# The last 96-point stage of an FFT filter in 64x64 tiles inside batched visits

## The chip, the cores and the metric

One core of one Trainium2 chip runs the kernel. The metric is device microseconds (us) of one execution. Every time below is in us unless it says ns. Engines are called as in the profile: PE or TensorE (matmul), PEld (its weight loads), DVE (VectorE), ACT (ScalarE), POOL (GpSimd) and SP (SyncE, which here only issues DMAs).

## The reference

```python
X = np.fft.rfft(x, axis=1)                  # x: 8 x 3072 x 256
y = np.fft.irfft(X * (filt_r + 1j * filt_i), n=3072, axis=1)
x = y.reshape(8 * 3072, 256)
h1, h2 = x @ w1, x @ w2                     # 256 -> 1024
out = np.maximum(h1, h2) @ w_out            # 1024 -> 256
```

The kernel uses max(h1, h2) = relu(x (w1 - w2)) + x w2, so the second part is out = relu(y Wd) Wo + y M with Wd = w1 - w2 and M = w2 w_out.

## The kernel before, in words

The transform of length 3072 is split as 96 x 32. For each of 8 batches there are four stages. s1 takes 96-point transforms along the first index, already as sums and differences of two halves of 48 (fold, on POOL, makes those from an fp32 load, load_xf); its result goes to DRAM (ad) and is read back transposed (bt, by s1_read). s2 does the 32-point part with the tables U, product multiplies by the filter on DVE, s3 goes back with the tables VP and VQ; its result goes to DRAM (zd) and is read back (zr, by z_read). s4 is the last stage, a 96-point transform for 4 of the 32 columns m, and makes one tile y_ of 384 points x 256 features, as two halves of 128 features. In before it is 8 matmuls of the stationary zr (96 x 128) with the moving table G1 (96 x 96).

The main loop runs over 64 tiles tt = 8 b + i, each of 8 steps j. A step has moe_h (two matmuls of 384 columns into one PSUM tile ph, and a ReLU into gt on ACT or DVE), and then 3 or 4 matmuls of moe_o for the tile before (into po, in another PSUM pool of two banks), whose result two blocks at a time is copied to ot on DVE and sent to DRAM by two DMAs on POOL's queue. **A step is named by its number 8 i + j in its batch, 0 to 63.** The tiles ph, pz, px, pa, py all come from one PSUM pool of six banks.

The order is written by hand and each engine keeps to it. While batch b goes through the loop, the stages s1 to s3 of later batches are done in visits, at steps listed by hand (mid: ahead of the step's moe_o; todo: behind it). A visit for number n does s3 of n-1, s2 of n, some s1 (a "quad" is one s1: four matmuls in 64x64 tiles of the array, a term I use for any such four), and the two products of n. plan_f2 lists, for each batch, the steps of the visits, of load_xf and fold, of both z_read (half h of the z rows) and of s1_read. s4(tt + 1) is called behind step 4 (6 for the last tile of a batch) of tile tt. SP's queue has all the DMAs of load_xf, s1 (ad), s1_read (bt), s3 (zd) and z_read (zr) in program order; a DMA that waits for data holds up those behind it.

In batch 0 the first stages are done in another way (s1t, t1, s3t, t2), with zr made by transposes.

Of the kernel before, what the change touches and what calls it, by code (L numbers as in the profile page):

```python
# [8 lines left out]
FP32 = mybir.dt.float32  # L9
BF16 = mybir.dt.bfloat16  # L10
AF = mybir.ActivationFunctionType
OP = mybir.AluOpType

B = 8
N = 3072
D = 256
# [4 lines left out]
NU = 24  # L21
TWO_PI = 6.283184
RND = 12582912.0


@with_exitstack
def kernel(
# [26 lines left out]
    M = const.tile([128, 2, D], BF16)  # L54
    I128 = const.tile([128, 128], BF16)
    NI = const.tile([128, 128], BF16)
    W1 = const.tile([128, 512], BF16)
    zT = const.tile([128, 2, NM, NU, 4], BF16)
    w2b = const.tile([128, 2, HID], BF16)
    w2T = const.tile([128, 8, D], BF16)  # L60

# [284 lines left out]
    def s1(b, c):  # L346
        if c == 0:
            ad[b] = dram.tile([96, NM, D], BF16, tag="ad", name="ad")
        if c % 2 == 0:
            at_[b] = apool.tile([128, 8, D], BF16, tag="at", name="at")  # L350
        at = at_[b]
        pa = [ps.tile([128, 2, D], FP32, tag="ps", name="pa%d" % g) for g in range(2)]
        for g, r in ((0, 0), (1, 1), (0, 1), (1, 0)):
            TE.matmul(pa[g][64 * r:64 * r + 64], CT[64 * g:64 * g + 64, r], xb[b, c][64 * g:64 * g + 64, r],  # L354
                      start=True, stop=True)
        for g in range(2):
            m0 = 4 * (c % 2) + 2 * g
            S.activation(at[:, m0:m0 + 2], pa[g], AF.Copy)  # L358
        if c % 2 == 1:
            for r in range(2):  # L360
                nc.sync.dma_start(out=ad[b][48 * r:48 * r + 48, 4 * c - 4:4 * c + 4], in_=at[64 * r:64 * r + 48])
# [6 lines left out]

    def z_read(b, h):
        if h == 0:  # L370
            zr[b] = zrpool.tile([96, NM, D], BF16, tag="zr", name="zr")
        src = zd[b][12 * h:12 * h + 12].rearrange("u (q m) d -> (u q) m d", q=4)
        for m in range(0, NM, 8):
            nc.sync.dma_start(out=zr[b][48 * h:48 * h + 48, m:m + 8], in_=src[:, m:m + 8])

    def s2(b, v):
        px = [ps.tile([128, 2, D], FP32, tag="ps", name="px%d" % s) for s in range(2)]
# [20 lines left out]
    def s3(b, v, pq):  # L398
        if v == 0:
            zd[b] = dram.tile([NU, 128, D], BF16, tag="zd", name="zd")  # L400
        pz = [ps.tile([128, 2, D], FP32, tag="ps", name="pz%d" % g) for g in range(2)]
        for i in range(2):
            for q, tab in enumerate((VP, VQ)):
                for g, s in ((0, 0), (1, 1), (0, 1), (1, 0)):
                    TE.matmul(pz[g][64 * s:64 * s + 64, i], tab[64 * g:64 * g + 64, 2 * v + i, s],  # L405
                              pq[s][64 * g:64 * g + 64, q, i], start=(q == 0), stop=(q == 1))
        zt = zpool.tile([128, 2, 2, D], BF16, tag="zt", name="zt")
        for g in range(2):
            S.activation(zt[:, :, g], pz[g], AF.Copy)  # L409
        nc.sync.dma_start(out=zd[b][4 * v:4 * v + 4].rearrange("u p d -> p u d"),  # L410
                          in_=zt.rearrange("p i g d -> p (i g) d"))
# [3 lines left out]
    def visit(b, n, quads):  # L415
# [7 lines left out]
        if n < 6:  # L423
            pend[b, n] = [product(V, n, s, px[s]) for s in range(2)]

    yt = {}

    def s4(tt):
        b, i = divmod(tt, 8)
        y_ = ypool.tile([128, 2, 384], BF16, tag="yt", name="y_")  # L430
        for dc in range(2):
            py = ps.tile([128, 4, NP], FP32, tag="ps", name="py")
            for m in range(4):
                TE.matmul(py[:, m], zr[b][:, 4 * i + m, 128 * dc:128 * dc + 128], G1, start=True, stop=True)  # L434
            o_ = y_[:, dc].rearrange("p (t m) -> p t m", m=4)
            i_ = py.rearrange("p m t -> p t m")
            if dc == 0:
                S.activation(o_, i_, AF.Copy, scale=1.0 / 1536.0)
            else:
                V.tensor_scalar(o_, i_, 1.0 / 1536.0, None, OP.mult)  # L440
        yt[tt] = y_
# [3 lines left out]
            if (j in (1, 4, 6) if 2 < 8 * i + j < 11 else j in (1, 2, 4, 6, 7) if 8 * i + j < 22  # L445
                else (j in (1, 5) and (i, j) != (3, 1)) or (i, j) == (3, 0) if 8 * i + j < 48 else j in (1, 3, 6))}

    def moe_h(tt, j):
        if j == 0:
            gt[tt] = gpool.tile([128, 8, 384], BF16, tag="gt", name="gt")  # L450
        y_ = yt[tt]
        ph = ps.tile([128, 384], FP32, tag="ps", name="ph")
        for dc in range(2):
            TE.matmul(ph, Wd[:, dc, 128 * j:128 * j + 128], y_[:, dc], start=(dc == 0), stop=(dc == 1))  # L454
        if (tt, j) in on_v if tt < 8 else j in (1, 3, 6):
            V.tensor_scalar(gt[tt][:, j], ph, 0.0, None, OP.max)  # L456
        else:
            S.activation(gt[tt][:, j], ph, AF.Relu)  # L458
# [14 lines left out]
    def moe_o(tt, k0, k1):  # L473
        y_, g_ = yt[tt], gt[tt]
        for k in range(k0, k1):
            c, e = divmod(k, 10) if tt else FIRST[k]
            n = e if tt else (e + 2) % 10
            q = 3 * tt + c
            blk = slice(128 * c, 128 * c + 128)
            if e == 0 and (q % 2 == 0 or q == 24 * B - 1):  # L480
                po[q // 2 % 2] = pso.tile([128, 2, D], FP32, tag="po", name="po")
            p_ = po[q // 2 % 2][:, q % 2]
            if n < 2:
                TE.matmul(p_, y_[:, n, blk], M[:, n], start=(e == 0), stop=(e == 9))  # L484
            else:
                TE.matmul(p_, g_[:, n - 2, blk], Wo[:, n - 2], start=(e == 0), stop=(e == 9))  # L486
            if e == 9 and q >= 24 * B - 2:
                e = q % 6
                if q % 2 == 0:
                    S.activation(ot[tt // 2][:, e], p_, AF.Copy)  # L490
                else:
                    S.activation(ot[tt // 2][:, e, 0:112], p_[:, 0:112], AF.Copy)
                    V.tensor_copy(ot[tt // 2][:, e, 112:D], p_[:, 112:D])
                out_block(tt, c)
            elif e == 9 and q % 2 == 1:
                if q % 6 == 1:
                    ot[tt // 2] = opool.tile([128, 6, D], FP32, tag="ot", name="ot")
                e = q % 6
                V.tensor_copy(ot[tt // 2][:, e - 1:e + 1], po[q // 2 % 2])  # L499
                for qq in (q - 1, q):  # L500
                    out_block(qq // 3, qq % 3)

# [80 lines left out]
    for c in range(8):  # L583
# [5 lines left out]
        if c < 7:  # L589
            spin(2)  # L590
    bt[0] = bpool.tile([128, NU, D], BF16, tag="bt", name="bt")
    for n in range(6):
        t1(n, S if n % 2 else V)
    put_v(0, 0, table_v(0, 0))
# [60 lines left out]
    apool = ctx.enter_context(tc.tile_pool(name="apool", bufs=3))  # L655
    zpool = ctx.enter_context(tc.tile_pool(name="zpool", bufs=3))
    opool = ctx.enter_context(tc.tile_pool(name="opool", bufs=2))
    ypool = ctx.enter_context(tc.tile_pool(name="ypool", bufs=3))
    gpool = ctx.enter_context(tc.tile_pool(name="gpool", bufs=2))
    f1(1, 0, S)  # L660
    spin(1)
# [10 lines left out]
    def plan(b, step, fn, *a):  # L672
        todo.setdefault((b + step // 64, step % 64), []).append((fn, a))
# [8 lines left out]
    def plan_f2(b, steps, quads, xs, folds):  # L682
        for n, st in enumerate(steps):
            mid.setdefault((b, st), []).append((visit, (b + 1, n, quads[n])))
        plan(b, steps[3] + 3, z_read, b + 1, 0)
        plan(b, steps[6] + 3, z_read, b + 1, 1)
        if b + 2 < B:
            for c in range(8):
                plan(b, xs[c], load_xf, b + 2, c)
                plan(b, folds[c], fold, b + 2, c)  # L690
            plan(b, steps[-1] + (6 if b else 11), s1_read, b + 2)
# [4 lines left out]
    for c, n in ((2, 7), (4, 22), (5, 32), (6, 40), (7, 48)):  # L696
        plan(0, n, t2, c, (V,))
    plan_f1(0, 1, (5, 6, 7, 7, 10, 10, 11, 11, 12, 12, 13, 13), 14)
    plan_f2(0, (25, 28, 31, 35, 38, 42, 46), ((0,), (), (1,), (2,), (3,), (4,), (5, 6)),
            (8, 10, 15, 18, 21, 27, 30, 33), (16, 19, 25, 28, 31, 34, 38, 42))  # L700
    for b in range(1, B - 1):
        plan_f2(b, (14, 18, 23, 31, 34 if b < B - 2 else 35, 39, 47), ((0,), (1,), (2,), (3,), (4,), (5,), (6, 7)),
                range(-25, 31, 7), range(-14, 42, 7) if b > 1 else range(-15, 41, 7))

    mid[0, 50] = [(visit, (1, 7, (7,)))]

    mid[0, 8] = [(t2, (3, (V,))), (prep_t, (1,))]

    for tt in range(8 * B + 1):
        b, i = divmod(tt, 8)  # L710
        k = 0
        for j in range(8):
            step = 8 * i + j
            if tt < 8 * B:
                moe_h(tt, j)
            for fn, a in mid.get((b, step), ()):
                fn(*a)
            if tt > 0:
                n = 3 if j in (3, 7) else 4
                moe_o(tt - 1, k, k + n)  # L720
                k += n
            for fn, a in todo.get((b, step), ()):
                fn(*a)
            if j == (6 if i == 7 else 5 if tt == 3 else 4) and tt + 1 < 8 * B:
                s4(tt + 1)


# [28 lines left out]
```

## Time and profile before

| | us |
|---|---|
| median of 3 runs | 501.48 (499.88 to 501.93) |
| span of the profiled execution, first to last instruction | 499.6 |
| what the runs have around that span | 0.3 to 2.3, by the median 1.9 |
| TensorE busy in the span | 486.2 |
| DVE, ACT, POOL busy | 329.9, 309.0, 258.7 |
| steps 0 to 63 of batch 0, 1, 2 and 6 | 63.4, 57.5, 57.1, 55.3 |

The profiled execution's own time is not listed apart from its span, so the median stands for it. A timeline row has the start, the length, the engine, the line, the operation, the tiles written and read, the shape and the count of merged instructions; in brackets the idle time of its engine before it and what ended that. In the chain of waits a row is one piece of the chain that ended last. For a matmul the length is from its start to the landing of its result, and the next one starts long before that.

### The profile page before, as it was taken

How to read it: one execution, taken by the hardware profiler on the slowest of the kernel's cores; microseconds unless marked ns; L12 is line 12 of the kernel's file. 1: busy time of each engine (PE TensorE's matmuls, PEld its weight loads, DVE VectorE, ACT ScalarE, POOL GpSimd, SP SyncE). 2: the span in 40 equal slices, each digit the busy share in tenths (PEclk: the TensorE clock that was granted, in tenths of full speed). 3: DMA queues.
4: the chain of work that ended last, by engine and by line, in shares of the span. 5: the costliest groups of instructions: out<-in, count | busy, mean ns of one | idle time of the engine just before them, and what ended most of it. 6: DMA issues, size and time to landing. Idle time of an engine off the chain costs nothing.

```text
span 499.6 us, 13073 instructions
## 1 busy us (share of the span) xinstructions
PE 486.2 (97%) x5297; PEld 361.0 (72%) x5300; DVE 329.9 (66%) x515; ACT 309.0 (62%) x630; POOL 258.7 (52%) x342
## 2 busy tenths in 40 slices
PE   7689999999999999999999999999999999999996
PEld 3457767777777777777777777777777777777775
DVE  7786788458865578457865678557774588555552
ACT  5777478647774577646775577646676456544442
POOL 8795569637546584539547394438642221222220
PEclk9989999999999999999999999999999999999999
DMA  8989799997689768896489776896677625521112
GB/s 130 159 236 219 216 245 298 277 258 210 206 241 245 206 202 219 257 261 195 150 252 251 197 231 189 261 261 181 199 205 206 158 85 149 172 83 64 64 64 85
DMA packets 78046, 97.23 MB, mean 195 GB/s; under 512 B 8065, under 2 KB 54434, under 8 KB 77954
## 3 DMA queue, kind: packets, MB, share of 16 engines
q1 hardware_dynamic: 64786, 66.80, 50.5%
q0 software_dynamic: 13200, 29.60, 20.7%
q8 instruction: 41, 0.67, 0.6%
q14 instruction: 19, 0.16, 0.1%
HBM read 53.87 MB, written 47.19 MB: 202 GB/s over the span
## 4 chain that ended last, share of the span: by engine, by line
PE 83%; DMA 11%; POOL 3%; SPq 1%; DVE 1%; issue 1%; ACT 0%; POOLq 0%
PE po L486 32%; PE ph L454 30%; PE po L484 8%; PE pz L405 4%; PE py L434 4%; DMA zd<-zt 2%; DMA bt<-ad 2%; DMA WS<-in_moe_w_dram 2%; PE px L381 2%; PE pa L354 2%; DMA xb<-in_x_dram 2%; POOL F L121 1%; DMA ad<-at 1%; POOL xb L88 1%; DMA F<-in_filt_i_dram 1%; DMA zr<-zd 1%
## 5 line engine op out<-in xcount | busy, mean ns | idle before, releaser
L486 PE MATMUL po<-Wo,gt 128*128 128x256 bf16 x1536 | 261.1, 273 | 0.0
L458 ACT ACTIVATE gt<-ph 128x384 bf16<-128x384 f32 x321 | 157.6, 495 | 146.8 <-PE ph L454 145.7
L486 PEld LDWEIGHTS <-gt 128*128 128x128 bf16 x1536 | 146.0, 98 | 66.7 <-issue 12.0
L467 POOL DMA_DIRECT2D out_dram<-ot x186 | 102.7, 557 | 170.8 <-DVE ot L499 166.4
L456 DVE TENSOR_SCALAR gt<-ph 128x384 bf16<-128x384 f32 x191 | 104.5, 553 | 64.3 <-PE ph L454 60.7
L387 DVE TENSOR_TENSOR pq<-px,F 128x1024 bf16<-128x1024 f32 x91 | 106.9, 1219 | 26.4 <-PE px L381 26.2
L454 PEld LDWEIGHTS <-Wd 128*128 128x128 bf16 x1024 | 96.5, 98 | 12.2 <-issue 0.3
L103 POOL TENSOR_TENSOR xb<-XF 128x512 bf16<-128x512 f32 x48 | 61.2, 1275 | 52.8 <-DMA XF<-in_x_dram 52.0
L499 DVE COPY ot<-po 128x512 f32<-128x512 f32 x95 | 65.2, 686 | 24.9 <-PE po L486 24.8
L104 POOL TENSOR_TENSOR xb<-XF 128x512 bf16<-128x512 f32 x48 | 60.9, 1269 | 0.0
L358 ACT ACTIVATE at<-pa 128x512 bf16<-128x512 f32 x96 | 51.8, 612 | 4.6 <-PE pa L354 4.6
L409 ACT ACTIVATE zt<-pz 128x512 bf16<-128x512 f32 x84 | 45.6, 595 | 4.9 <-PE pz L405 0.8
L434 PE MATMUL py<-G,zr 96*128 96x96 bf16 x512 | 32.6, 206 | 0.1
L434 PEld LDWEIGHTS <-zr 96*128 96x128 bf16 x512 | 28.9, 97 | 2.4 <-DVE zr L563 0.6
L405 PE MATMUL pz<-pq,VP 64*64 64x256 bf16 x336 | 22.0, 281 | 0.0
L381 PE MATMUL px<-bt,U 64*64 64x256 bf16 x384 | 20.2, 278 | 1.3 <-ACT VQ L278 0.7
L405 PE MATMUL pz<-pq,VQ 64*64 64x256 bf16 x336 | 21.0, 269 | 0.0
L405 PEld LDWEIGHTS <-VP 64*64 64x64 bf16 x336 | 9.9, 105 | 13.3 <-issue 13.0
L354 PE MATMUL pa<-xb,CT 64*64 64x512 bf16 x192 | 18.1, 377 | 0.3 <-DVE y__1495 L440 0.3
L381 PEld LDWEIGHTS <-U 64*64 64x64 bf16 x384 | 10.5, 108 | 4.2 <-issue 3.6
L570 PE MATMUL pd<-W 128*128 128x512 bf16 x28 | 10.1, 474 | 1.5 <-DVE zero L149 1.5
L405 PEld LDWEIGHTS <-VQ 64*64 64x64 bf16 x336 | 10.0, 106 | 0.0
(428 smaller groups left out, 602.9 us busy)
## 6 DMA issues: line engine op xcount, KB each, us to landing
out_dram<-ot POOLq DMA_DIRECT2D x186, 128.0 KB, 3.7
XF<-in_x_dram SPq DMA_DIRECT2D x96, 192.0 KB, 4.6
ad<-at SPq DMA_DIRECT2D x56, 192.0 KB, 3.7
zd<-zt SPq DMA_DIRECT2D x42, 256.0 KB, 3.1
zr<-zd SPq DMA_DIRECT2D x56, 192.0 KB, 4.6
bt<-ad SPq DMA_DIRECT2D x13, 768.0 KB, 10.5
WS<-in_moe_w_dram SPq DMA_DIRECT2D x4, 512.0 KB, 8.1
xb<-in_x_dram POOLq DMA_DIRECT2D x8, 192.0 KB, 6.6
```

What stands on the lines that cost most here:

```text
L103: G.tensor_tensor(t_[:, 0], f[:, 0], f[:, 1], OP.add)
L104: G.tensor_tensor(t_[:, 1], f[:, 0], f[:, 1], OP.subtract)
L358: S.activation(at[:, m0:m0 + 2], pa[g], AF.Copy)
L387: E.tensor_tensor(pq, px.rearrange("p (o i) d -> p o i d", o=1).to_broadcast([128, 2, 2, D]), F[:, :, 2 * v:2 * v + 2, s], OP.mult)
L405: TE.matmul(pz[g][64 * s:64 * s + 64, i], tab[64 * g:64 * g + 64, 2 * v + i, s], pq[s][64 * g:64 * g + 64, q, i], start=(q == 0), stop=(q ...
L434: TE.matmul(py[:, m], zr[b][:, 4 * i + m, 128 * dc:128 * dc + 128], G1, start=True, stop=True)
L454: TE.matmul(ph, Wd[:, dc, 128 * j:128 * j + 128], y_[:, dc], start=(dc == 0), stop=(dc == 1))
L456: V.tensor_scalar(gt[tt][:, j], ph, 0.0, None, OP.max)
L458: S.activation(gt[tt][:, j], ph, AF.Relu)
L467: E.dma_start(out=dst, in_=ot[tt // 2][:, 3 * (tt % 2) + c])
L486: TE.matmul(p_, g_[:, n - 2, blk], Wo[:, n - 2], start=(e == 0), stop=(e == 9))
L499: V.tensor_copy(ot[tt // 2][:, e - 1:e + 1], po[q // 2 % 2])
```

## The change

s4 of tiles 8 to 63 becomes s4f. The 96 points are split into two halves of 48 (by the parity s of the frequency), which zr now holds on partitions 0 to 47 and 64 to 111; z_read writes them with two DMAs where there was one. Each half is transformed with a table G2 of 48 x 48, in 64x64 tiles of the array, 32 matmuls of 48 columns for a tile, into two PSUM tiles pc. ACT copies the one to ce, and DVE writes the sum and the difference of ce and the other to y_. The scale 1/1536 goes to the output copy. s4f is called in the visits (visit_y), ahead of s1, s3 and s2. A batch has ten visits from batch 2 on, at other steps than before; the steps of load_xf, fold, z_read and s1_read move as well, the ReLUs are dealt out anew between ACT and DVE (relu_on_v), and zT moves into the pool of bt. Batch 0 keeps s4 and its own plan, and gets table_g2 and a visit at step 61.

```diff
+SCALE = 1.0 / 1536.0
...
+    G2 = const.tile([128, 64], BF16)
     W1 = const.tile([128, 512], BF16)
-    zT = const.tile([128, 2, NM, NU, 4], BF16)
...
     def z_read(b, h):
         if h == 0:
-            zr[b] = zrpool.tile([96, NM, D], BF16, tag="zr", name="zr")
-        src = zd[b][12 * h:12 * h + 12].rearrange("u (q m) d -> (u q) m d", q=4)
+            zr[b] = zrpool.tile([128, NM, D], BF16, tag="zr", name="zr")
+        src = zd[b][12 * h:12 * h + 12].rearrange("u (s r m) d -> s u r m d", s=2, r=2)
         for m in range(0, NM, 8):
-            nc.sync.dma_start(out=zr[b][48 * h:48 * h + 48, m:m + 8], in_=src[:, m:m + 8])
+            for s in range(2):
+                nc.sync.dma_start(out=zr[b][64 * s + 24 * h:64 * s + 24 * h + 24, m:m + 8],
+                                  in_=src[s][:, :, m:m + 8])
...
+    def table_g2():
+        pg = ps.tile([128, 64], FP32, tag="ps", name="pg2")
+        for s in range(2):
+            TE.matmul(pg[64 * s:64 * s + 64], CT[0:64, s], I128[0:64, 0:64], start=True, stop=True)
+        S.activation(G2, pg, AF.Copy)
+
     yt = {}
+
+    def s4f(tt):
+        b, i = divmod(tt, 8)
+        y_ = ypool.tile([128, 2, 384], BF16, tag="yt", name="y_")
+        pc = [ps.tile([128, 2, 4, 48], FP32, tag="ps", name="pc%d" % s) for s in range(2)]
+        for dc in range(2):
+            for m in range(4):
+                for s, h in ((0, 0), (1, 1), (0, 1), (1, 0)):
+                    d0 = 128 * dc + 64 * h
+                    TE.matmul(pc[s][64 * h:64 * h + 64, dc, m], zr[b][64 * s:64 * s + 48, 4 * i + m, d0:d0 + 64],
+                              G2[64 * s:64 * s + 48, 0:48], start=True, stop=True)
+        ce = cepool.tile([128, 2, 48, 4], FP32, tag="ce", name="ce")
+        S.activation(ce, pc[0].rearrange("p c m t -> p c t m"), AF.Copy)
+        for k, op in enumerate((OP.add, OP.subtract)):
+            V.tensor_tensor(y_[:, :, 192 * k:192 * k + 192].rearrange("p c (t m) -> p c t m", m=4),
+                            ce, pc[1].rearrange("p c m t -> p c t m"), op)
+        yt[tt] = y_
+
+    def visit_y(b, n, tiles, quads):
+        for tt in tiles:
+            s4f(tt)
+        for c in quads[1:]:
+            s1(quads[0], c)
+        if n is not None and n > 0:
+            s3(b, n - 1, pend.pop((b, n - 1)))
+        if n is not None and n < 6:
+            px = s2(b, n)
+            pend[b, n] = [product(V, n, s, px[s]) for s in range(2)]
 
     def s4(tt):
         b, i = divmod(tt, 8)
@@ -445,6 +482,19 @@
             if (j in (1, 4, 6) if 2 < 8 * i + j < 11 else j in (1, 2, 4, 6, 7) if 8 * i + j < 22
                 else (j in (1, 5) and (i, j) != (3, 1)) or (i, j) == (3, 0) if 8 * i + j < 48 else j in (1, 3, 6))}
 
+    def relu_on_v(tt, j):
+        if tt < 8:
+            return (tt, j) in on_v
+        b, i = divmod(tt, 8)
+        step = 8 * i + j
+        if b == B - 1 or b == B - 2 and step > 43:
+            return j in (1, 3, 6)
+        if step < 3 or step > 42:
+            return j % 2 == 1
+        if b == 1 and step < 10:
+            return j % 2 == 1
+        return step in ((10, 15, 20, 26, 32, 37) if b == 1 else (3, 10, 16, 22, 28, 35, 40))
+
     def moe_h(tt, j):
         if j == 0:
             gt[tt] = gpool.tile([128, 8, 384], BF16, tag="gt", name="gt")
@@ -452,7 +502,7 @@
         ph = ps.tile([128, 384], FP32, tag="ps", name="ph")
         for dc in range(2):
             TE.matmul(ph, Wd[:, dc, 128 * j:128 * j + 128], y_[:, dc], start=(dc == 0), stop=(dc == 1))
-        if (tt, j) in on_v if tt < 8 else j in (1, 3, 6):
+        if relu_on_v(tt, j):
             V.tensor_scalar(gt[tt][:, j], ph, 0.0, None, OP.max)
         else:
             S.activation(gt[tt][:, j], ph, AF.Relu)
...
-                V.tensor_copy(ot[tt // 2][:, e - 1:e + 1], po[q // 2 % 2])
+                if tt < 8:
+                    V.tensor_copy(ot[tt // 2][:, e - 1:e + 1], po[q // 2 % 2])
+                else:
+                    V.tensor_scalar(ot[tt // 2][:, e - 1:e + 1], po[q // 2 % 2], SCALE, None, OP.mult)
...
+    zT = bpool.tile([128, 2, NM, NU, 4], BF16, tag="bt", name="zT")
...
-    ypool = ctx.enter_context(tc.tile_pool(name="ypool", bufs=3))
+    ypool = ctx.enter_context(tc.tile_pool(name="ypool", bufs=4))
+    cepool = ctx.enter_context(tc.tile_pool(name="cepool", bufs=2))
...
+    mid[0, 50] = [(visit, (1, 7, (7,)))]
+    plan(0, 44, table_g2)
+    mid[0, 61] = [(visit_y, (1, None, (8,), ()))]
+
+    def at(b, st, tiles=(), quads=(), n=None):
+
+        if b + st // 64 >= 0:
+            mid.setdefault((b + st // 64, st % 64), []).append((visit_y, (b + 1, n, tiles, quads)))
+
     for b in range(1, B - 1):
-        plan_f2(b, (14, 18, 23, 31, 34 if b < B - 2 else 35, 39, 47), ((0,), (1,), (2,), (3,), (4,), (5,), (6, 7)),
-                range(-25, 31, 7), range(-14, 42, 7) if b > 1 else range(-15, 41, 7))
-
-    mid[0, 50] = [(visit, (1, 7, (7,)))]
+        t = 8 * b
+        nb = b + 2 if b + 2 < B else None
+        if b == 1:
+            at(b, 4, (t + 1,), (3, 0, 1))
+            at(b, 10, (t + 2,), (3, 2), 0)
+            at(b, 15, (), (3, 3), 1)
+            at(b, 20, (t + 3,), (), 2)
+            at(b, 26, (t + 4,), (), 3)
+            at(b, 32, (t + 5,), (), 4)
+            at(b, 37, (), (3, 4), 5)
+            at(b, 43, (t + 6,), (3, 5), 6)
+            at(b, 47, (), (3, 6, 7))
+            z0, z1, read = 30, 46, 52
+            folds = range(-15, 41, 7)
+        else:
+            early = b == 2
+            s3_, s22, s40 = ((nb, 3), (nb, 4), (nb, 5)) if early else ((nb, 4), (nb, 5), ())
+            at(b, 3, (t + 1,), s3_ if nb else (), 0)
+            at(b, 10, (t + 2,), (), 1)
+            at(b, 16, (t + 3,), (), 2)
+            at(b, 22, (), s22 if nb else (), 3)
+            at(b, 28, (t + 4,), (), 4)
+            at(b, 35, (t + 5,), (), 5)
+            if nb:
+                at(b, 40, (), s40, 6)
+                at(b, 43, (t + 6,), (nb, 6, 7))
+            else:
+                at(b, 43, (t + 6, t + 7), (), 6)
+            z0, z1, read = 26, 44 if nb else 46, 49
+            folds = range(-23, 33, 7) if early else range(-31, 25, 7) if b == 3 else range(-35, 29, 8)
+        if nb:
+            more = b + 3 < B
+            first = b + 1 == 2
+            at(b, 51, (t + 7,), ((b + 3, 0) if first else (b + 3, 0, 1)) if more else ())
+            at(b, 59, (t + 8,), ((b + 3, 1, 2) if first else (b + 3, 2, 3)) if more else ())
+        else:
+            at(b, 59, (t + 8, t + 9))
+        plan(b, z0, z_read, b + 1, 0)
+        plan(b, z1, z_read, b + 1, 1)
+        if nb:
+            for c in range(8):
+                plan(b, folds[c] - 11, load_xf, nb, c)
+                plan(b, folds[c], fold, nb, c)
+            plan(b, read, s1_read, nb)
+    for k in (2, 4, 6):
+        at(B - 1, 8 * k - 5, (8 * B - 8 + k, 8 * B - 7 + k))
...
             if j == (6 if i == 7 else 5 if tt == 3 else 4) and tt + 1 < 8 * B:
-                s4(tt + 1)
+                if tt + 1 < 8:
+                    s4(tt + 1)
```

More of the change, by code (lines that the diff above doesn't have):

```diff
@@ L489, in moe_o @@
                 if q % 2 == 0:
-                    S.activation(ot[tt // 2][:, e], p_, AF.Copy)
+                    S.activation(ot[tt // 2][:, e], p_, AF.Copy, scale=SCALE)
                 else:
-                    S.activation(ot[tt // 2][:, e, 0:112], p_[:, 0:112], AF.Copy)
-                    V.tensor_copy(ot[tt // 2][:, e, 112:D], p_[:, 112:D])
+                    S.activation(ot[tt // 2][:, e, 0:112], p_[:, 0:112], AF.Copy, scale=SCALE)
+                    V.tensor_scalar(ot[tt // 2][:, e, 112:D], p_[:, 112:D], SCALE, None, OP.mult)
                 out_block(tt, c)
```

## The prediction

> **What bounds the kernel now.** I read the page first, parts 1 and 4.
>
> ```profile
> PE 486.2 (97%) x5297; PEld 361.0 (72%) x5300; DVE 329.9 (66%) x515; ACT 309.0 (62%) x630; POOL 258.7 (52%) x342
> PE 83%; DMA 11%; POOL 3%; SPq 1%; DVE 1%; issue 1%; ACT 0%; POOLq 0%
> ```
>
> TensorE is busy for 97% of the span and carries 83% of the chain. The view by windows says where it isn't: in the steady batch from 159.0 to 216.1 it is busy for 57.10 us of 57.10, at clock 1.00. DVE has 38.07 there and ACT 37.12. So from batch 1 on every microsecond of TensorE work, and every wait put in front of it, moves the end; ACT and DVE count only through when they free something. Next, the timeline of TensorE around one visit and one s4 (start, length; a matmul's length is latency, its cost is the distance to the next start):
>
> ```profile
> 230.77 0.49 PE L454 MATMUL ph<-y__4292,Wd 128*128 128x384 bf16 x2
> 231.19 0.30 PE L405 MATMUL pz<-pq,VP 64*64 64x256 bf16 x4
> 231.32 0.28 PE L405 MATMUL pz<-pq,VQ 64*64 64x256 bf16 x4
> 231.65 0.39 PE L381 MATMUL px<-bt,U 64*64 64x256 bf16 x8
> 231.87 0.39 PE L354 MATMUL pa<-xb,CT 64*64 64x512 bf16 x4
> 232.19 0.39 PE L486 MATMUL po<-Wo,gt 128*128 128x256 bf16 x2
> ...
> 234.05 0.51 PE L434 MATMUL py<-G,zr 96*128 96x96 bf16 x8
> 234.39 0.49 PE L454 MATMUL ph<-y__4292,Wd 128*128 128x384 bf16 x2
> ```
>
> An s4 costs 0.34 (234.05 to 234.39). A visit pays for the change of tile form: the ph pair takes 0.33, so the first pz was due at 231.10 and came 0.09 late; its first four take 0.13 where later fours take 0.11; the pa quad takes 0.215, so po was due at 232.085 and came 0.10 late. That is 0.22 a visit. s3 is 0.46, later 0.44 (without the 0.02), s2 0.22, one s1 0.22.
>
> Small 64x64 tiles stand in the start-up, also at clock 1.00:
>
> ```profile
> 18.70 0.38 PE L264 MATMUL pv<-I,U 64*64 64x64 bf16 x24
> 18.91 0.27 PE L381 MATMUL px<-bt,U 64*64 64x256 bf16 x1
> ```
>
> Six quads with 64 moving columns take 0.21: 35 ns a quad.
>
> **The change, part by part.** Scale: the profiled execution has a span of 499.6, the median of the runs is 501.48, so 1.9 lies around the span; I put differences on the median.
>
> *TensorE's own work.* 56 tiles (8 to 63) give up an s4 of 0.34 for 8 quads of 48 columns. Upper price 35 ns a quad (L264's row, wider by a third): 0.28. Lower: two px quads of 256 columns take 0.22, so 0.43 ns a column, 21 ns a quad, 0.17. I take L264 by its columns, 48/64 x 35 = 26 ns, 0.21, since that row has the tile form. Gain 56 x 0.13 = 7.3 (3.4 to 9.5). Against it, visits go from 50 (8 + 6 x 7) to 71 (9, 11, 4 x 10, 8, 3 by batch): 21 x 0.22 = 4.6, and table_g2 changes form once more, 0.2. Sum -2.5 (+1.4 to -4.7). The Trainium skill, "TensorE: Matmul & The Clock Gate", section LDWEIGHTS, gives a weight load as columns over 1.2 per ns, 53 ns for 64, and "TensorEngine Tiling (Array Packing)", Gotcha 2, denies fast weight load to column tiles; at 53 ns a quad an s4f would be 0.43 by estimate and the change would lose on TensorE alone. L264's 35 ns, with a fresh 64-column load for each matmul, disagrees.
>
> *ACT and DVE.* An s4 is one ACT and one DVE pass of 128x384; an s4f is one on ACT (0.49) and two on DVE (0.55 by L440; the operand from SBUF is new, but the product L387 has such an operand and takes 1.22 for 1024 elements, the same rate). In batches 2 to 5, ReLUs on DVE go from 24 to 19. DVE: 38.07 + 8 x 0.55 - 5 x 0.55 = 39.7; ACT 37.12 + 5 x 0.49 = 39.6, of 57. The scale moved into the output copy replaces a copy of the same shape. Nothing here, by sum.
>
> *PSUM banks.* There are six. A visit now often takes seven tiles with the ph of its step still in one (ph + 2 pc + 4 more), so the last waits for the first to come free: that ph, whose ReLU these visits have on DVE. How long that takes, after an output copy:
>
> ```profile
> 103.83 0.49 PE L454 MATMUL ph<-y__2135,Wd 128*128 128x384 bf16 x2
> 103.81 0.69 DVE L499 COPY ot<-po 128x512 f32<-128x512 f32 x1 [0.36 <-PE po L486]
> 104.42 0.55 DVE L456 TENSOR_SCALAR gt<-ph 128x384 bf16<-128x384 f32 x1
> ```
>
> From the start of ph to the end of its ReLU 1.14; a visit starts 0.42 after ph (230.77 to 231.19); with 0.05 for the signal the bank is free 0.77 into the visit, without the copy 0.70. A tile and two more pairs need it at 0.23 + 0.22 = 0.45; a tile, s3 and s2 at 0.23 + 0.44 = 0.67; a quad, s3 and s2 at 0.68. Waits: 8 visits at 0.25 (step 43 of batches 1 to 5, step 59 of 2 to 4), 6 at 0.32 behind a copy (3, 51), 5 at 0.10 (35), 18 at 0.03, 6 at 0.02, and 0.2 at step 4 of batch 1: 5.2 in all. Today the visits that take seven have that ReLU on ACT (ends 0.59 in) and need the bank at 0.68, so they don't wait. Ends: 0, and 7.5 if DVE comes 0.07 later each time.
>
> *The read of bt by batch 1.* The chain of waits:
>
> ```profile
> 94.91 0.32 SPq L374
> ...
> 97.21 5.09 DMA ad<-at
> 102.33 0.03 issue
> 102.36 10.96 DMA bt<-ad
> 113.32 0.04 issue
> 113.37 0.41 PE px L381 x7
> ```
>
> SP's queue waits for zd, issues four z reads (94.91 to 96.77, 1.86), then ad, then bt, and TensorE already stands about 0.4 for bt at step 14. The change asks at step 10: 3.28 earlier (ph of step 14 starts at 112.56, of step 10 at 109.28), so at 109.70, later by table_g2 0.2, the visit at 61 0.1 (0.43 less an s4), that at step 4 0.7, and 0.45 of this visit: 111.2. And the read comes later: z_read by parity issues eight DMAs for four, with ad and bt behind them on SP, +1.9: 115.2. Wait 4.0, less today's 0.4: +3.6. Ends: 0.6 (no delay, and landing in the 9.8 that is bt's median) and 4.6.
>
> *The fold for step 59 of batch 1.* Chunk 2 of batch 4 is folded in step 55, behind that step's output DMAs on POOL:
>
> ```profile
> 154.01 1.12 POOL L467 DMA_DIRECT2D out_dram<-ot  x2 [0.56 <-DVE ot L499]
> 155.15 1.28 POOL L103 TENSOR_TENSOR xb<-XF 128x512 bf16<-128x512 f32 x1
> 156.37 1.27 POOL L104 TENSOR_TENSOR xb<-XF 128x512 bf16<-128x512 f32 x1
> ```
>
> These are the output DMAs of step 55; a fold ends at 157.64. Step 59's ph starts at 155.10, its visit at 155.52, its second quad is due at 155.97: +1.7 (0 to 1.7). The other folds come in time by the same count, some by 0.2 only.
>
> *The read of bt by batch 2.* From the visit at step 43 of batch 1: the last zd goes out after 3.2 (1.9 now; ce and two pa now stand ahead of it on ACT), lands 3.1 later, eight z reads 4.5 (twice 1.86 or 2.64), two ad 1.0 and 3.7 to land, bt 0.5 and 9.8: 25.8. Step 3 of batch 2 asks after 24 steps of 0.73 (0.33 for ph, 3.75 po at 0.109), visits of 1.4, 0.65, 0.7, 2.6 and its own 0.45: 23.3. Wait 2.5 (0 to 4). From batch 2 on the last quads are at step 43 with s3 at 40; the same sum leaves 2 to 4 us to spare.
>
> Sum: -2.5 + 5.2 + 3.6 + 1.7 + 2.5 = +10.5: **512.0**.
>
> **Rivals.** *Faster: TensorE's own work is all that counts*, since other work covers each new wait: -2.5 and today's 0.4 give 498.6, at 21 ns a quad 496.4. It decides from the point where bt lands before 111.2 and a visit's ReLU frees its bank before 0.45. For it: DVE and ACT have a third of the time free. Against: bt landed at 113.32 with four fewer DMAs ahead of it on SP. 0.14. *Reads on time, banks short:* -2.5 + 5.2 = 504.2; for it, landings of bt range from 3.7 to 14.0. 0.12. *Banks no limit, reads late:* 512.0 - 5.2 = 506.8; for it, TensorE waits hardly at all now with the same six banks. 0.16. *The clock falls:* after TensorE was busy for 1.77 of the 3.5 us to 23.0, the granted clock was 0.50 from 23.0 to 29.8; a wait of 4.0 at step 10 could do this again, and 6.8 us at half clock cost 3.4: 515.4. Against: the waits of today's batches cost no clock, but none is over 0.5. 0.14. The Trainium skill, same page on the clock gate, Part 1, has the clock halved after an idle window of about 3.4 us on a free-running grid, which a wait of 4.0 need not cover; the trace's fall after a half-idle stretch agrees in kind. *Weight loads bound the quads*, each load waiting for the one before on its part of the array: L539's quick run of loads with 64 moving columns has one every 53 ns in the stretch at half clock, and at that price an s4f is 0.43, +0.09 x 56 = +5.0 in place of -7.3: 524.3. Against: the same line comes every 29 ns once the clock is 1.00, and L264. 0.04.
>
> **How the numbers follow.** The forecast has 0.40. Leaving out the faster case and the weight loads (0.18), the range goes from below 504.2, by the cheaper quads, to above 515.4, by the dearer banks and reads: 500 to 518. About 0.5% (2.5 us) is what a measurement of this kernel can tell from no change. Faster 0.14; within it 0.08 (the lower part of the second rival); slower 0.78.
>
> **What would show it.** Right: pc quads 26 ns apart and an s4f near 0.21; px at step 10 of batch 1 waiting some 4 us for bt<-ad; pa at step 59 of batch 1 waiting for POOL; gaps of 0.25 to 0.3 ahead of the last pair of seven-tile visits, released by DVE's ReLU; the form change 71 times at 0.22. Wrong: a steady batch (2 to 5) shorter than 57.1 us, or batch 1 without a long wait; then the banks or the reads were misjudged. If a batch from 3 on waits for bt, the margins were.

## The result, and the profile after

The changed kernel takes **545.91** (median of 4 runs, 544.15 to 549.87) against 500.76 for the kernel before in the same comparison: ratio 1.0905, 95% interval 1.0854 to 1.0957. The forecast was 512.0 with 518 as its upper end: the direction was right, the size four times too small. The profiled execution took 549.87, with a span of 547.8.

The page after, part 1 (busy time), the granted clock from part 2, and the head of part 4 (the chain):

```profile
PE 506.7 (93%) x6643; PEld 360.8 (66%) x6646; DVE 343.0 (63%) x541; ACT 322.2 (59%) x661; POOL 258.7 (47%) x342
PEclk9799999889999699997999889997999999999999
PE 68%; DMA 14%; SPq 8%; ACT 4%; issue 2%; POOL 2%; DVE 1%; POOLq 0%
```

TensorE carries less of the chain: its share falls from 83% to 68%, while SP's queue goes from 1% to 8%, ACT from 0% to 4% and DMA from 11% to 14%. And the clock, which was full after the start-up, has holes. The view by windows, a batch a row (length, busy time of each engine with counts, clock, DMA share):

```profile
105.70:171.80 66.10, 61.24 (x813) 42.69 (x812) 41.01 (x62) 40.65 (x85) 35.14 (x42) 0.97 0.77 210
171.80:240.00 68.20, 62.07 (x806) 43.28 (x805) 39.78 (x60) 40.35 (x83) 35.65 (x43) 0.92 0.72 198
240.00:305.50 65.50, 61.10 (x802) 42.92 (x801) 39.77 (x60) 39.48 (x81) 32.94 (x41) 0.95 0.68 193
434.20:491.00 56.80, 55.76 (x802) 41.51 (x801) 39.35 (x59) 33.31 (x69) 13.00 (x25) 1.00 0.41 126
```

Batches 1 to 4 take 65 to 68 where they took 57; batch 6, which has no s1 and hence no loads of XF, takes 56.8 where it took 55.3. The waits view names who held TensorE and, in its last row here, its weight loads:

```profile
PE pa L355 <- POOL xb L104: 11.7, 4, 4.0
PE px L384 <- DMA bt<-ad: 10.7, 4, 4.7
PE pc L445 <- DMA zr<-zd: 3.1, 2, 1.6
PEld L355 <- DVE gt L506: 4.2, 11, 0.7
```

Now a place where nothing waits, the visit of step 10 in batch 3, on TensorE's timeline:

```profile
255.85 0.49 PE L504 MATMUL ph<-y__4719,Wd 128*128 128x384 bf16 x2
256.27 0.44 PE L445 MATMUL pc<-G,zr 48*64 48x48 bf16 x32
256.54 0.28 PE L408 MATMUL pz<-pq,VP 64*64 64x256 bf16 x4
```

From the first pc to the first pz it is 0.27: 0.02 for the form and 8 quads at 32 ns. Step 3 of the same batch, where it does wait:

```profile
242.32 0.49 PE L504 MATMUL ph<-y__4584,Wd 128*128 128x384 bf16 x2
242.74 0.44 PE L445 MATMUL pc<-G,zr 48*64 48x48 bf16 x32
246.94 0.58 PE L355 MATMUL pa<-xb,CT 64*64 64x512 bf16 x1 [3.76 <-POOL xb L104]
248.16 0.64 PE L355 MATMUL pa<-xb,CT 64*64 64x512 bf16 x3 [0.64 <-POOL xb L105]
...
250.41 1.06 PE L536 MATMUL po<-Wo,gt 128*128 128x256 bf16 x4
```

The quad of s1 waits 4.7 in all for the fold. Behind the wait four po take 0.85 to the next start where they took 0.44: half clock, until 253.1. The chain of waits says where the fold's delay came from:

```profile
226.64 0.77 SPq L376
...
233.73 0.98 SPq L368
...
234.81 3.40 SPq L94
...
238.26 7.21 DMA XF<-in_x_dram
...
246.85 1.27 POOL xb L105
```

Eight reads of z (L376) hold SP's queue from 226.64 to 233.02; the read of bt (L368) follows; the load of XF for the fold of step 61 (L94) stands next, its issue is held for 3.40, it lands at 245.5, and POOL then folds.

I added up, from the matmul starts in the trace, by how much each start is later than the one before it allows, from the first ph of batch 1 to the last matmul:

| | before | after |
|---|---|---|
| the last stage's matmuls (py; pc) | 18.8 | 15.2 |
| changes of tile form | 8.2 | 12.1 |
| waits over 0.2 | 0.4 | 30.5 |
| matmuls at half clock, the excess | 0 | 11.9 |
| all other work and gaps | 366.4 | 368.1 |
| sum | 393.8 | 437.8 |

Of the 30.5: bt at step 10 of batch 1 3.9; the fold at step 59 of batch 1 1.8; step 3 of batch 2 6.9 (0.5 for the fold, then bt); the folds at step 3 of batches 3, 4 and 5 4.7, 5.0 and 4.4; bt at step 3 of batch 6 1.3; banks, 11 times 0.22 to 0.28, 2.6 (ten of them are at a pa whose weight load the profile has waiting for a ReLU on DVE, gt L506). Batch 0 adds 3.4 for zr at step 61, and 1.3 at half clock.

### The profile page after: what moved, and what is told of

It is laid out like the page before. It is cut to its first block, busy times and chain, and to the rows that moved or that the text cites. A ratio compares the mean times of both kernels' runs of the same rounds, so it can differ in the third digit from the quotient of the medians.

```text
span 547.8 us, 15976 instructions
## 1 busy us (share of the span) xinstructions
PE 506.7 (93%) x6643; PEld 360.8 (66%) x6646; DVE 343.0 (63%) x541; ACT 322.2 (59%) x661; POOL 258.7 (47%) x342
## 4 chain that ended last, share of the span: by engine, by line
PE 68%; DMA 14%; SPq 8%; ACT 4%; issue 2%; POOL 2%; DVE 1%; POOLq 0%
PE po L536 25%; PE ph L504 23%; DMA bt<-ad 6%; PE po L534 6%; SPq L376 5%; DMA XF<-in_x_dram 4%; PE pz L408 4%; PE pc L445 3%; PE px L384 2%; SPq L94 2%; ACT at L359 2%; DMA ad<-at 1%; PE pa L355 1%; POOL xb L105 1%; DMA xb<-in_x_dram 1%
## 5 line engine op out<-in xcount | busy, mean ns | idle before, releaser
L536 PE MATMUL po<-Wo,gt 128*128 128x256 bf16 x1536 | 267.5, 278 | 0.0
L508 ACT ACTIVATE gt<-ph 128x384 bf16<-128x384 f32 x351 | 172.1, 495 | 143.6 <-PE ph L504 141.0
L536 PEld LDWEIGHTS <-gt 128*128 128x128 bf16 x1536 | 147.9, 99 | 69.7 <-issue 16.6
L506 DVE TENSOR_SCALAR gt<-ph 128x384 bf16<-128x384 f32 x161 | 89.1, 554 | 97.1 <-PE ph L504 96.4
L504 PEld LDWEIGHTS <-Wd 128*128 128x128 bf16 x1024 | 101.3, 99 | 14.7 <-issue 0.3
L552 DVE TENSOR_SCALAR ot<-po 128x512 f32<-128x512 f32 x83 | 56.9, 685 | 32.7 <-PE po L536 32.4
L448 ACT ACTIVATE ce<-pc 128x384 f32<-128x384 f32 x56 | 26.9, 490 | 35.3 <-PE pc L445 35.3
L355 PE MATMUL pa<-xb,CT 64*64 64x512 bf16 x192 | 23.1, 401 | 14.8 <-POOL xb L104 11.7
L384 PE MATMUL px<-bt,U 64*64 64x256 bf16 x384 | 24.2, 295 | 11.8 <-DMA bt<-ad 10.7
L445 PEld LDWEIGHTS <-zr 48*64 48x64 bf16 x1792 | 18.6, 109 | 19.4 <-issue 15.2
L445 PE MATMUL pc<-G,zr 48*64 48x48 bf16 x1792 | 24.0, 189 | 3.1 <-DMA zr<-zd 3.1
L355 PEld LDWEIGHTS <-CT 64*64 64x64 bf16 x192 | 7.1, 107 | 24.3 <-issue 16.7
L408 PEld LDWEIGHTS <-VP 64*64 64x64 bf16 x336 | 10.2, 107 | 3.6 <-issue 3.5
## 6 DMA issues: line engine op xcount, KB each, us to landing
WS<-in_moe_w_dram SPq DMA_DIRECT2D x4, 512.0 KB
```

Of the source, the lines that this page charges most:

```text
L445: TE.matmul(pc[s][64 * h:64 * h + 64, dc, m], zr[b][64 * s:64 * s + 48, 4 * i + m, d0:d0 + 64], G2[64 * s:64 * s + 48, 0:48], start=True, ...
L552: V.tensor_scalar(ot[tt // 2][:, e - 1:e + 1], po[q // 2 % 2], SCALE, None, OP.mult)
```

## The experiments

The theories: **Q**, the reads of z hold SP's queue; **S**, the load of XF stands behind the read of bt; **P**, the visits stand too early, so that bt is asked for too soon; **C**, the clock falls because TensorE idles; **B**, the banks.

### Two and four reads of z a half

```diff
-        for m in range(0, NM, 8):
-            for s in range(2):
-                nc.sync.dma_start(out=zr[b][..., m:m + 8], in_=src[s][:, :, m:m + 8])
+        for s in range(2):                   # e2: range(0, NM, 16), m:m + 16
+            nc.sync.dma_start(out=zr[b][...], in_=src[s])
```

This is the kernel with two reads. The one with four keeps both loops, with m in steps of 16.

> The changed kernel, but each half of z is read by two DMAs (all 32 columns m at once) in place of eight; the same bytes. Theory Q (the queue): in the changed kernel eight reads hold SP's queue for 6.4 us (0.80 each, 0.75 of it issue), and the read of bt and the loads XF stand behind them; so TensorE waits 4 to 7 us at step 3 of batches 2 to 5, and the clock falls behind each wait. With two reads (1.6) the queue is free 4.8 earlier, the waits at step 3 fall from 5 to under 1, and the clock stays: 510 to 520. Rival P (the place): the visits were moved too early, and bt and the folds would be late whatever the number of reads: over 538.

Measured 542.49, ratio 1.083 (1.0778 to 1.0881): Q alone, as I stated it, fails, and the time is the one that P gave. For bt alone Q is borne out: by the sum from the matmul starts, the wait at step 10 of batch 1 falls from 3.9 to 0.2, and that for bt at step 3 of batch 2 from 6.4 to 2.1.

> The changed kernel, but four reads of z a half (16 columns m each) in place of eight. Theory Q: 3.2 us on the queue in place of 6.4, waits at step 3 about 2 to 3 in place of 5, under the length that lowers the clock: 520 to 530, between the changed kernel and the one with two reads. Rival P: over 540.

Measured 536.86, ratio 1.071 (1.0664 to 1.0756): better than two, and less than Q wanted. SP's timeline of the kernel with two reads shows what stayed:

```profile
219.97 1.60 SPq L375 DMA_DIRECT2D zr<-zd  x2
221.67 1.58 SPq L368 DMA_DIRECT2D bt<-ad  x2
223.30 8.24 SPq L94 DMA_DIRECT2D XF<-in_x_dram  x2
```

The reads did shrink from 6.4 to 1.6 and bt did go out earlier, but the two loads of XF behind it were then held for 8.2 in place of 3.9. Counted from the first read of z they go out only 0.5 earlier, and TensorE still waits for folds (13.9 in all, 16.4 in the changed kernel). With two reads the first columns of z also land later: the waits for zr grow from 3.4 to 8.3. The price of one read is, by the median, 0.75 to 0.79 of issue whether it moves 4, 8 or 16 KB to a partition.

### Eight reads in the kernel before

```diff
+            for k in (0, 24):
+                nc.sync.dma_start(out=zr[b][48 * h + k:48 * h + k + 24, m:m + 8], in_=src[k:k + 24, m:m + 8])
```

> The kernel before, but with eight reads of z a half (24 partitions each) in place of four; nothing else changes. It asks for bt only at step 14. Theory Q with the price by form: these reads have one stride over the partitions, as before, and cost 0.45 to 0.5 each, 3.7 a half; the wait for bt in batch 1 grows from 0.4 to about 2 and later batches have room: 502 to 504. If the number of DMAs alone made the 0.8, a half takes 6.4 and batch 1 waits 4 to 5: 505 to 507. Rival P: the number of reads matters little in either kernel: 501 to 502.

Measured 501.80, ratio 1.0011 (0.9996 to 1.0026): no difference. SP's timeline of this kernel:

```profile
207.08 3.67 SPq L375 DMA_DIRECT2D zr<-zd  x8
211.40 1.54 SPq L367 DMA_DIRECT2D bt<-ad  x2
```

Eight reads take 3.67, by the median 0.36 of issue each. So it is not the number that costs 0.75 but the form: in the changed kernel the DRAM side has two strides over the 24 partitions (u and r), here one. The wait in batch 1, which I had put at 2, did not grow.

### Spare work in the waits

```diff
+        if 3 <= b <= 6 and n == 0:
+            spin(14)
         for c in quads[1:]:
```

> The changed kernel with 14 spare matmuls of 512 columns (3.0 us) on TensorE at step 3 of batches 2 to 5, ahead of the s1 that waits there for the fold; their result isn't used. Theory: it is the idle time that halves the clock; these fill it, the four stretches of 6.8 to 10 us at half clock behind step 3 go, and 2.5 to 3.4 us a batch come back: 533 to 538. If the clock falls for another reason, or the waits move along with the spare work, 545 to 558.

Measured 542.80, ratio 1.083 (1.0775 to 1.0885). The view by windows around step 3 of batches 2 and 3, first the changed kernel, then this one (the clock is the third number from the end; around step 3 of batches 4 and 5 it is 0.76 and 1.00):

```profile
174.00:190.00 16.00, 9.87 (x86) 5.80 (x85) 5.22 (x7) 4.51 (x10) 5.02 (x7) 0.68 0.82 212
242.00:256.00 14.00, 9.60 (x90) 5.95 (x88) 5.22 (x7) 4.90 (x10) 6.51 (x7) 0.76 0.71 215
```

```profile
174.00:190.00 16.00, 14.44 (x185) 9.36 (x184) 7.93 (x13) 7.35 (x15) 9.86 (x12) 1.00 0.92 248
242.00:256.00 14.00, 12.38 (x145) 8.52 (x144) 7.43 (x9) 7.41 (x15) 9.64 (x10) 1.00 0.59 201
```

C holds as a mechanism: with the wait filled, the clock stays at 1.00 in all four. At step 61 of batch 0 and step 10 of batch 1, where nothing fills the wait, it falls as in the changed kernel. The gain was to be 8 to 13; by medians it is 3.1. The profiled executions differ by 10.4 (549.87 and 539.48), but other runs reached 546.29, so how much of the 11.9 comes back in a typical run stays open.

### XF loaded earlier, alone and with four reads

```diff
-                plan(b, folds[c] - 11, load_xf, nb, c)
+                plan(b, folds[c] - 15, load_xf, nb, c)
```

> The changed kernel, with each load of XF in batches 1 to 6 issued 15 steps ahead of its fold in place of 11. Theory S (the load behind bt): the load for the fold of step 61 (step 50 before) stands right behind the read of bt (step 49) on SP's queue, and there its issue is held for 3 to 8 us; at step 46 it stands ahead of that read. Then the fold is done by step 67, the waits of 5 us at step 3 of batches 3, 4 and 5 go, and with them three stretches of 6.8 at half clock: 8 us each, 520 to 526. Theory Q (the eight reads of z): the load is then behind the reads of z instead, and comes as late: 540 to 547.

Measured 534.13, ratio 1.0615 (1.0557 to 1.0673), less of a gain than S wanted. The waits of 4 to 5 for the fold at step 3 of batches 3 to 5 are gone, as S says, but the visit then waits 1.0 to 2.2 for bt, and 3.5 in batch 2, and the wait at step 10 of batch 1 grows from 3.9 to some 6. Its waits view:

```profile
PE px L384 <- DMA bt<-ad: 12.4, 6, 4.1
PE pc L445 <- DMA zr<-zd: 3.7, 1, 3.7
```

> Both: four reads of z a half, and XF loaded 15 steps ahead. Theory S and Q together: waits are left at step 61 of batch 0 (2.5), at step 59 of batch 1 (1.6) and at step 3 of batch 2 (3 to 4), 8 in all where the changed kernel has 31: 511 to 518. If either alone explains it, the same as that one alone.

Measured 520.04, ratio 1.0371 (1.0321 to 1.042), 2 over what I had expected. Four reads alone give 9.1, the earlier load alone 11.8, both 25.9: together they give 5 more than the two apart, so one wait had hidden another. Left, by the waits view, are 3.9 for bt and 3.1 for zr.

### The price of a quad

```diff
-        pc = [ps.tile([128, 2, 4, 48], FP32, ...
-                              G2[64 * s:64 * s + 48, 0:48], start=True, stop=True)
+        pc = [ps.tile([128, 2, 4, 64], FP32, ...
+                              G2[64 * s:64 * s + 48], start=True, stop=True)
```

> The changed kernel with 64 moving columns in each matmul of s4f in place of 48 (16 of them zero columns, not used). If the quads of 48 columns at 31.7 ns are held by something other than their columns (the load of 64 weight columns, or the issue), they stay at 31.7 and the time at 544 to 549. If the columns set the price, they go to about 40 ns, 56 x 8 x 8 ns = 3.8 us, some of it in waits: 548 to 551.

Measured 547.22 (median of three runs), ratio 1.0909 (1.0874 to 1.0944), as the changed kernel. A visit's quads on this kernel's TensorE timeline:

```profile
254.31 0.45 PE L445 MATMUL pc<-G,zr 48*64 48x64 bf16 x32
254.59 0.28 PE L408 MATMUL pz<-pq,VP 64*64 64x256 bf16 x4
```

0.28 for 64 columns, 0.27 for 48, and the single starts lie 32 ns apart in both. A third more columns cost nothing, so 48 columns don't set the price. Whether the load of the 64 weight columns does, or something else in a quad, was not tried.

### s4f in the place of s4

```diff
-                s4(tt + 1)
+                (s4 if tt + 1 < 8 else s4f)(tt + 1)
```

on the kernel before, with G2, ce, the scale in the output copy and four reads of z by parity.

> The kernel before, its own schedule, with s4f called where s4 was for tiles 8 to 63 (outside the visits, so each pays its own change of tile form), four reads of z a half, the scale in the output copy, ReLUs as before. By the rows: 8 quads at 31.7 and 0.02 are 0.27 in place of 0.34, -0.07 x 56 = -3.8; 56 changes of form at 0.22, +12.3; the longer issue of the reads of z, +1 at step 14 of batch 1: +9.5, 510 to 512. If the schedule of the change and not its parts is what costs, that is 1.02 of before at most; if s4f itself or its work on ACT and DVE made TensorE wait, 520 and more.

Measured 519.55, ratio 1.0371 (1.0327 to 1.0415). The same sum as above, from batch 1 on: last stage -3.4, changes of form +10.7, waits +10.1, half clock 0 (1.5 in the start-up). I had missed the waits: 7.4 of them are the first ph of each batch, for which TensorE waits 1.06 because y_ now comes through ACT and then DVE. So in the place of s4, s4f pays for the form each time and, for the first tile of a batch, comes too late; the visits are there for both.

### A shared ReLU, z by parity in DRAM, and all together

```diff
+            V.tensor_scalar(gt[tt][:, j, 0:192], ph[:, 0:192], 0.0, None, OP.max)
+            S.activation(gt[tt][:, j, 192:384], ph[:, 192:384], AF.Relu)
```

at the crowded visits, on the kernel of 520.04:

> Four reads of z, XF 15 steps ahead (the kernel of 520.0), and at the steps whose visit takes seven banks early (4, 10, 43, 59 of batch 1; 3, 43, 51, 59 of 2 to 5) the ReLU of that step's ph is shared, 192 columns on DVE and 192 on ACT. Theory B (banks): the last pair of such a visit starts 0.7 to 0.77 into the visit because it waits for that ReLU; a half ends some 0.2 earlier, so 17 waits shrink by about 0.2 each: 3 us less, 515.5 to 518.5. Rival: the gap there is the array's own (the change between lines), and nothing moves: 519 to 521.

Measured 521.36, ratio 1.0401 (1.0348 to 1.0455): no gain, and near the rival's number. But the edit did not do what it was to do: ACT's half was not done beside DVE's but after it (ACT's and DVE's timelines, step 51 of batch 3):

```profile
274.68 0.35 DVE L507 TENSOR_SCALAR gt<-ph 128x192 bf16<-128x192 f32 x1
275.06 0.33 ACT L508 ACTIVATE gt<-ph 128x192 bf16<-128x192 f32 x1 [0.72 <-DVE gt L507]
```

So the bank came free later: ACT's half ends at 275.39, the last pair of pa starts at 275.44, and the waits at these places grew from 0.22 and 0.28 to 0.39 and 0.44. The edit failed as a remedy and answered its question: the gap follows the end of the ReLU, not the array. Why ACT's half waited for DVE's was not tried.

```diff
-            zd[b] = dram.tile([NU, 128, D], ...)         # one write of 128 partitions
+            zd[b] = dram.tile([2, NU, 64, D], ...)       # two writes of 64 partitions
...
+                src = zd[b][s, 12 * h:12 * h + 12].rearrange("u (r m) d -> (u r) m d", r=2)
```

> The kernel of 520.0 with z kept in DRAM by parity, so that each read of z has one stride over its 24 partitions (two writes of 64 partitions in place of one of 128). Theory F (form): a read then takes 0.36 on SP as in the kernel before with eight reads, not 0.76; a half 1.6 in place of 3.3; bt lands 1.7 earlier and the waits at step 61 of batch 0 and step 3 of batches 2, 5 and 6 (3.4, 2.8, 2.0, 0.5) shrink by 4 to 6 in all: 514 to 517. Rival: the two reads of z that wait for zd, not their issue, set the time, and the added writes cost as much: 519 to 522.

Measured 520.80, ratio 1.0391 (1.0362 to 1.042), the rival's number. The reads of a half took 1.95 in place of 3.3 in one such place, and the waits for bt didn't shrink (by the sum from the matmul starts, 9.9 in the profiled run, 5.5 in that of the kernel of 520.04). The form sets the price here too, by the median 0.36 a read. But each of the two writes of z takes 0.61 where the one took 0.39, so the run doesn't tell whether the reads' issue has stopped to matter or the added writes ate the gain.

```diff
+            at(b, 40, (), (3, 5, 6))
+            at(b, 43, (t + 6,), (3, 7), 6)
-            at(b, 47, (), (3, 6, 7))
...
+            folds = (-25, -18, -12, -5, 2, 9, 16, 23) if early else ...
...
+    mid[0, 62] = [(visit_y, (1, None, (8,), ()))]
```

> All of it (parity in DRAM, four reads, XF 15 steps ahead, shared ReLUs), and in batch 1 quads 5 and 6 at step 40 with quad 7 at 43 in place of step 47, the folds of batch 4 two or three steps earlier, the first s4f at step 62. If waits and clock are all that is left of the loss, the account is: s4f -3.8, 21 changes of form +4.6, table_g2 +0.2, the shared ReLUs' visits 1 to 2, waits left 2 to 4: 505 to 509. That it comes out under 501 isn't expected by any theory here, since the quads and the changes of form cancel. Over 512: a cost is missing in the account.

Measured 522.92, ratio 1.0448 (1.0415 to 1.0481). It misses 505 to 509 by far, so the account lacked something: the shared ReLUs cost, and 8.5 of waits for bt are left, one in every batch from 1 to 6. In this kernel's chain of waits, ahead of batch 4, one read of bt took 16.6:

```profile
271.20 1.97 ACT at L359 x4
...
277.59 16.63 DMA bt<-ad
```

The view by windows, first over that read and then over the read of bt of 10.9 in the kernel before (102.36 in the prediction's chain):

```profile
277.60:294.20 16.60, 15.02 (x181) 9.91 (x172) 9.01 (x18) 10.79 (x24) 12.12 (x15) 1.00 1.08 272
```

```profile
102.40:113.30 10.90, 10.88 (x95) 8.12 (x93) 5.93 (x11) 5.12 (x11) 3.55 (x4) 1.00 1.09 247
```

The last two numbers are the DMA share and GB/s. In both the share is full, and by length times GB/s 4.5 MB are moved while the longer read lasts and 2.7 while the shorter one does. So when bt lands seems to depend also on what else is moved meanwhile; no theory here had this, and no run varied it on its own.

### The place of the visits

In the changed kernel with four reads, the earlier load and shared ReLUs, s2 one visit later (n = 0 at step 10, n = 5 at 40, quads 6 and 7 at 47, s1_read at 52, z_read at 31 and 46). The ReLUs of steps 3 and 43 of batches 2 to 5 are no longer shared:

```diff
-            at(b, 3, (t + 1,), s3_ if nb else (), 0)
-            at(b, 10, (t + 2,), (), 1)
+            at(b, 3, (t + 1,), s3_ if nb else ())
+            at(b, 10, (t + 2,), (), 0)
...
+                at(b, 47, (), (nb, 6, 7))
```

> The kernel with four reads of z, XF 15 steps ahead and shared ReLUs (521.4), with s2 of batches 2 to 6 one visit later: n = 0 at step 10 in place of 3, n = 5 at 40, quads 6 and 7 at a visit of their own at 47, s1_read at 52, z_read at 31 and 46. Theory P (the place): what is left are waits for bt at step 3, which asks 18 steps after the read is issued; at step 10 it has 22, and these waits (0.7 to 2.5 in batches 2 to 6 by the run) go, with any clock lost behind them; the added visit costs 0.22 in four batches: 514 to 518. Rival: bt comes later by as much as it is asked for later, since SP's queue holds it: 520 to 523.

Measured 517.05 (514.67 to 517.9), ratio 1.0303 (1.026 to 1.0346), against 521.36 (517.61 to 523.37) for its parent: a small gain, and part of it can come from the two ReLUs a batch that are no longer shared. The waits for bt in batches 2 to 6, by the sum 2.9 in the parent's profile, are gone from its waits view; what remains is zr in batch 0 (2.7), the fold at step 59 of batch 1 (1.8), 0.5 for the fold at step 3 of batches 2 to 5, and bank waits, lengthened by the shared ReLU. Its span is still 15.7 over that of the kernel before. Of these, 5.3 lie in batch 0, and of the 10.5 from batch 1 on, waits over 0.2 are 7.4 and half clock 1.0.

And the place alone, in the kernel before:

```diff
-        plan_f2(b, (14, 18, 23, 31, 34 if b < B - 2 else 35, 39, 47), (
+        plan_f2(b, (14, 18, 23, 28, 33, 38, 43) if b == 1 else (3, 10, 16, 22, 28, 35, 43), (
```

> The kernel before, all its parts as they are, but the visits of batches 2 to 6 at the places of the change (3, 10, 16, 22, 28, 35, 43; batch 1 at 14, 18, 23, 28, 33, 38, 43), z_read and s1_read following them (25, 46, 49), folds and loads unmoved. If the place alone makes bt late: waits of 1 to 4 us at step 3 of batches 2 to 6 and the clock with them, 506 to 520. If the place is harmless while SP's queue has four cheap reads of z (1.9 us a half) and no load of XF that a near step needs: bt has 18 to 19.5 of 19.7 us, 501 to 504.

Measured 515.03, ratio 1.0267 (1.0228 to 1.0306). The last stage, the banks' owners, the ReLUs and the form and number of the reads of z are those of before (z_read and s1_read move with the visits), and it loses 13.7. Its waits view:

```profile
PE px L381 <- DMA bt<-ad: 5.2, 5, 1.8
```

By the sum from the matmul starts, waits for bt at the first visit of batches 1 to 5 are 6.6, short waits of ph behind visits 3.1, half clock 1.5. P holds: asking for bt 18 steps after its read is too soon in either kernel, by 0.8 to 2.1 in batches 2 to 5 here; batch 6 does not wait.

## Why the prediction was wrong

**TensorE's own work: a term mis-sized.** Predicted -2.5 (quads at 26 ns, 56 x 0.13 = 7.3 gained; form 4.8 lost). Measured -3.6 for the last stage and +3.9 for the form: about nothing. The step that failed is "I take L264 by its columns, 48/64 x 35". The row itself, without the scaling, gave 32 ns a quad (35 with the change of form in it), and that is what 48 columns take. With it the change has nothing to win before any wait. The Trainium skill, "TensorE: Matmul & The Clock Gate", section LDWEIGHTS, gives a weight load as its columns over 1.2 per ns, by estimate 53 ns for 64. The runs have a quad, with its four loads, every 32 ns, so quads don't follow one another at that price here; whether loads overlap or are shorter, no run shows.

**Banks: the mechanism right, the sum too large.** Predicted 0.25 at steps 43 and 59 and 0.32 behind a copy at 51; measured 0.22 and 0.28, released by DVE's ReLU as forecast. The sum is 2.6 in waits over 0.2, with some of the 1.7 of other gaps, for 5.2 predicted; those of step 3 don't show, since the fold or bt held TensorE longer there.

**The fold at step 59: right**, 1.7 predicted and 1.8 measured. **bt at batch 1: the number right by luck**, 4.0 predicted and 3.9 measured. The forecast had bt land at 115.2 and TensorE ask for it at 111.2. bt landed at 119.2, since its zd landed 2.3 later than before and the eight reads took 6.4, not the 3.8 of the forecast (its ad, for its part, landed 1.0 faster). TensorE asked at 115.4, since batch 1 began 4.1 later than in the kernel before. Two misses of the same size cancel.

**zr at step 61 of batch 0: a term left out.** The visit there was priced at 0.1 of work. It waits 3.4 for zr, with 1.3 of half clock behind it, and no term of the sum had a wait there.

**bt and the fold at step 3: the main miss.** I had 2.5 for batch 2 and nothing from batch 3 on; measured 6.9, then 4.7, 5.0, 4.4 and 1.3. Two steps failed. First, "eight z reads 4.5 (twice 1.86 or 2.64)": they take 6.4, since a read with two strides costs 0.75 of issue and not the 0.42 of the row I doubled. The diff shows the second stride, and no row of the trace had that form; I should have bounded it from above and not by the row of another form. Second, "the other folds come in time by the same count, some by 0.2 only": I counted from POOL's side, with the load of XF taken as landed. But the load was planned for step 50, one behind the read of bt at 49, and the profile of before shows that the load behind that read is held: 5.79 in one place, in this row of SP's timeline of the kernel before, which I had read and not used.

```profile
154.53 5.79 SPq L93 DMA_DIRECT2D XF<-in_x_dram  x1
```

And the margin of "2 to 4 us to spare" for bt from batch 2 on was none: the place alone, with the cheap reads, made TensorE wait 0.8 to 2.1 for bt in batches 2 to 5.

**The clock: a rival made too small.** I gave it one stretch, 3.4, at 0.14. There were four waits of 4 to 7 beside that of step 10, and half clock from 178.0 for 10.2, from 246.2, 311.1 and 375.9 for 6.8 each, from 102.9 (in batch 0) and 119.9 for 3.4 each: 11.9 of excess from batch 1 on. All are multiples of 3.41, and so, within 0.02, are the times between their starts. The Trainium skill, same page, Part 1, has a window of 3413 ns that runs freely; the trace agrees, with these lengths and starts beside it.

From batch 1 on the loss is 44.0: 22.3 at step 3, 11.9 of half clock, 5.3 for bt at step 10 and the fold at step 59 (less today's 0.4), 2.6 for banks, 0.3 of TensorE's own work and 1.7 of other gaps. Batch 0 and what stands ahead of it add 4.1.

## What to carry to other kernels

Where TensorE is busy all the time, a wait costs its length and can cost up to 3.4 more in clock: in these runs every wait of 3.5 and more was followed by half clock, and of those of 1.8 to 2.8 some were and some not. So a schedule that asks earlier for data must be priced on the queue that brings it: every DMA ahead of it, at the issue price of its own access form, and every DMA behind a large strided read. A move of visits should be tried alone, with the old parts, before parts are changed with it. And a small matmul's price should be taken from a row as it stands, not scaled by columns that may not set it.

## What the runs showed of the hardware

- A quad of 64x64 tiles with fresh weights takes 32 ns with 48 and with 64 moving columns.
- A DMA's issue on SP takes, by the median, 0.75 to 0.79 when its DRAM side has two strides over the 24 partitions, with 4, 8 or 16 KB a partition; 0.36 (24 partitions) to 0.42 (48) with one stride.
- The DMA behind a read of bt (two DMAs of 64 partitions x 24 runs of 512 bytes) is held at issue: two loads of XF for 3.88 (3.40 of it the first) in the changed kernel, for 8.24 with two reads of z ahead in place of eight. Why, no run shows.
- While a read of bt is under way the DMA engines are full (share 1.08 and 1.09 in the rows above), and it took 10.9 with 247 GB/s moved and 16.6 with 272.
- Waits of 2.1 (the place alone, at 343.3; two reads, at 176.7) were followed by 3.4 at half clock, waits of 2.6 and 2.7 (step 3 of batch 2 in the kernels of 520.04 and 536.86) by none. All stretches at half clock in the changed kernel begin multiples of 3.41 apart.
